# Strassen's seven products in a second group of tokens, weight sums taken from fp16, and two transposes copied out by ScalarE

## Chip, cores and metric

The kernel runs on one core of one Trainium2 chip. The metric is the time of one execution on the device, in microseconds (us). A core has TensorE (PE) for matmuls, VectorE (DVE), ScalarE (ACT) and GpSimd (POOL) for elementwise work, and SyncE (SP), which here only issues DMAs. Each engine works through its own queue in order.

## The reference

Two layers follow each other: a causal attention without softmax, with a decay per head, and a two-layer network with a gelu.

```python
# q, k, v: (4, 8, 768, 64); blocks of 64 positions, a state kv per head
intra = einsum('bhic,bhjc->bhij', qb, kb) * Dmask
out   = einsum('bhij,bhjd->bhid', intra, vb) + einsum('bhid,bhde->bhie', qb * lam_pow, kv_state)
kv_state = lam_block * kv_state + einsum('bhsd,bhse->bhde', kb_dec, vb)
# x: the attention's output as (3072, 512); w_in (512, 2048), w_out (2048, 512)
h = x @ w_in
g = gelu_tanh(h)
return g @ w_out            # (3072, 512), float32
```

## The kernel before, in words

**Attention in 24 steps.** A step is 256 positions of four heads of one batch. `prep(s)` scales q (DVE, L225), casts k (ACT, L230) and scales v (POOL, L215) into fp16. `stage_t(s)` transposes q and k on PE (L246) and copies the PSUM tile to SBUF: on ACT for steps 1, 5 and 6 (L253), half and half for 2 and 3, on DVE for 0, 4, 7 and 8 (L255). From step 9 on, a DMA transposes, and `stage_t` does nothing. `R(n, s)` computes the scores of step n (L275), then K-state and output products of n and s (L310, L324, L333), copies the output to `xT` on ACT (L352), masks the scores on DVE (`causal`, L284) and updates the state: `t` on DVE (L372 or L369), from which POOL makes `u` (L379). `U(n)` is the second update of a step.

**The network in 7 groups.** A superblock is two steps, 256 tokens. Groups are `[0,1], [2], [3], [4,5], [6,7], [8,9], [10,11]`: group 0 has 512 tokens, groups 1 and 2 have 256, the others 512. The first product (L407, in group 0 also L522) makes 128 columns of h at a time, and ACT writes their gelu to `gT` (L411). For the second product there are two forms. `mm2` (L422, groups 0 and 1) is the plain one: sixteen matmuls of 512 columns for each 128 tokens. `product` (L476, groups 2 to 6) is Strassen's scheme: tokens, the hidden dimension and the output columns are each halved, and seven products of sums take the place of eight, each of eight matmuls of 256 columns for each 128 tokens of a half. Its inputs are five sums of `gT` blocks (`sum_g`, DVE, L452), five sums of w_out blocks made once (`sum_wout`, DVE, L123), and plain blocks. Products come in the order 3, 4, 5, 2, 1, 7, 6; 3 and 4 need no sum of g. After product 2, ACT copies PSUM out (L483, L484) and DVE combines (L487, L488); after 1 and 6, DVE adds to it (L496, L508), and SP sends the rows out.

**The order is written out by hand.** `pin` keeps program order on every engine. `queue_group` (called in `R` when a group's last step is done) appends pieces of a group to the list `filler`: a piece is one `mm1` call, one `mm2` call or one `product`. `fill(n)` emits the next n pieces, so that attention steps and pieces alternate; the calls from L606 on set where. `behind(k, i0, i1)` hangs `sum_g` for rows i0 to i1 on piece k of a group, in program order just after it. Group 1's pieces (eight of `mm1`, eight of `mm2`) come out from the `fill(1)` behind `prep(8)` to the `fill(3)` of the loop's n = 9; group 2's follow.

**Weights.** w_out is loaded as fp32 into four staging tiles (tag `w32`, which the sums of g use later), cast to `w_out16` by POOL and ACT (`cast_wout`), and `sum_wout` reads the fp32 staging tiles: the half j = 0 before `fill(8)`, the half j = 1 in the loop at n = 8, 9 and 10.

Of the kernel before, what the change touches and what calls it, by code (L numbers as in the profile page):

```python
# [15 lines left out]
def kernel(  # L16
# [11 lines left out]
    pin = tc.keep_in_program_order  # L28
# [32 lines left out]
    def load_step(s):  # L61
# [3 lines left out]
        for nm, src in (("q", q), ("k", k), ("v", v)):  # L65
# [8 lines left out]
    w_out16 = w16p.tile([P, NF, DM], FP16)  # L74


    HF, HE = NF // 2, DM // 2
    w_sum16 = w16p.tile([P, 5, HF, HE], FP16)
    W_SUMS = {3: ((0, 1), ALU.subtract, (1, 1)), 4: ((1, 0), ALU.subtract, (0, 0)),
              1: ((0, 0), ALU.add, (1, 1)), 7: ((1, 0), ALU.add, (1, 1)),  # L80
              6: ((0, 0), ALU.add, (0, 1))}
    w_slot = {m: i for i, m in enumerate(W_SUMS)}
    wstage = {}
# [25 lines left out]
    def cast_wout(j, eng):  # L109
        t = wstage[("o", j)]  # L110
        for i in range(2):
            dst = w_out16[:, 4 * j + 2 * i : 4 * j + 2 * i + 2, :]
            src = t[:, 2 * i : 2 * i + 2, :]
            if eng[i] is nc.scalar:
                pin(nc.scalar.activation(out=dst, in_=src, func=AF.Copy))
            else:
                pin(nc.gpsimd.tensor_copy(out=dst, in_=src))

    def sum_wout(j, m, eng):

        (f0, e0), op, (f1, e1) = W_SUMS[m]
        a, b = wstage[("o", j + 2 * f0)], wstage[("o", j + 2 * f1)]
        pin(eng.tensor_tensor(w_sum16[:, w_slot[m], 4 * j : 4 * j + 4, :],  # L123
                              a[:, :, e0 * HE : e0 * HE + HE], b[:, :, e1 * HE : e1 * HE + HE], op))


    lam_in = const.tile([P, H], FP32)
# [74 lines left out]
    def prep(s):  # L202
        prep_qk(s)
        prep_v(s)
# [8 lines left out]
    def prep_v(s):  # L213
        tv = a16p.tile([P, 2, HH, D], FP16, tag="v16", name=f"v16_{s}")
        pin(nc.gpsimd.tensor_tensor(wide(tv[:]), ld32[s][2][:], decay(dv, s), ALU.mult))  # L215
        a16[s] = a16[s] + (tv,)
        if s >= 6:
            load_ahead(s + 3)

    def prep_qk(s):  # L220
        q32, k32, _ = ld32[s]
        tqk = a16p.tile([P, 2, 2, HH, D], FP16, tag="qk16", name=f"qk16_{s}")
        tq, tk = tqk[:, 0], tqk[:, 1]
        q_eng = nc.gpsimd if s == 3 else nc.vector
        pin(q_eng.tensor_tensor(wide(tq), q32[:], decay(dq, s), ALU.mult))  # L225
        if s == 0:
            inverse(halves[0])
            odd(halves[1])
            inverse(halves[1])
        pin(nc.scalar.activation(out=wide(tk), in_=k32[:], func=AF.Copy))  # L230
        a16[s] = (tq, tk)
        if s >= FIRST_DMA_T:
            o = qkp.tile([P, 2, 2, 2, P], FP16, tag="qkT", name=f"qkT_{s}")
            pin(nc.sync.dma_start_transpose(out=o[:].rearrange("p a j h t -> p (a j h) t"),
                                            in_=tqk[:].rearrange("p a j h d -> p (a j h d)")))
            qkT[s] = o

    def stage_t(s):
        if s >= FIRST_DMA_T:
            return  # L240
        tq, tk = a16[s][:2]
        Tps = ps_M.tile([P, 2, 2, 2, P], FP16, tag="M", name="Tps")
        for i, t in enumerate((tq, tk)):
            for hp in range(2):
                for j in range(2):
                    pin(nc.tensor.transpose(Tps[:, i, j, hp, :], t[:, j, 2 * hp : 2 * hp + 2, :],  # L246
                                            ident[:]))
        o = qkp.tile([P, 2, 2, 2, P], FP16, tag="qkT", name=f"qkT_{s}")
        if s in (2, 3):
            pin(nc.scalar.activation(out=o[:, 0], in_=Tps[:, 0], func=AF.Copy))  # L250
            pin(nc.vector.tensor_copy(out=o[:, 1], in_=Tps[:, 1]))
        elif s in (1, 5, 6):
            pin(nc.scalar.activation(out=o[:], in_=Tps[:], func=AF.Copy))  # L253
        else:
            pin(nc.vector.tensor_copy(out=o[:], in_=Tps[:]))  # L255
        qkT[s] = o
# [131 lines left out]
    filler = []  # L388

    def queue_group(g):  # L390
        N = len(groups[g]) * SB
        NTAU = N // P
# [10 lines left out]
        def mm1(fs):  # L403
            Hps = ps_M.tile([P, per, N], FP32, tag="M", name="Hps")
            for i, f in enumerate(fs):
                for c in range(NC):
                    pin(nc.tensor.matmul(by_block(Hps[:, i, :]), w_in16[:, c, f * P : (f + 1) * P],  # L407
                                         x(c), start=(c == 0), stop=(c == NC - 1)))
            f = fs[0]
            dst = gT[:, f, :, :] if per == 2 else gT[:, f % HF, f // HF : f // HF + 1, :]  # L410
            pin(nc.scalar.activation(out=dst, in_=Hps[:], func=AF.Gelu_apprx_tanh))  # L411
# [4 lines left out]
        def mm2(tau, part):  # L416

            if not O2.get(tau):
                O2[tau] = [ps_M.tile([P, DM], FP32, tag="M", name="O2ps"), 0]
            for f in range(4 * part, 4 * part + 4):  # L420
                n = O2[tau][1]
                pin(nc.tensor.matmul(O2[tau][0][:], gT[:, f % HF, f // HF, tau * P : (tau + 1) * P],  # L422
                                     w_out16[:, f, :], start=(n == 0), stop=(n == NF - 1)))
                O2[tau][1] += 1
            if O2[tau][1] < NF:
                return
            o32 = otp.tile([P, DM], FP32, tag="o32", name="o32")
            pin(nc.scalar.activation(out=o32[:], in_=O2.pop(tau)[0][:], func=AF.Copy))
            pin(nc.sync.dma_start(out=out[row0 + tau * P : row0 + tau * P + P, :], in_=o32[:]))
# [11 lines left out]
        def block(T, F, i):  # L441
            return gT[:, i, F, T * HN : (T + 1) * HN]

        def sum_g(i0, i1):
            for m, ((T0, F0), op, (T1, F1)) in G_SUMS.items():
                if m not in gsum:
                    k = len(gsum)
                    if k % 2 == 0:
                        pairs.append(wst.tile([P, 2, HF, HN], FP16, tag="w32", name=f"gs_{g}_{m}"))
                    gsum[m] = pairs[-1][:, k % 2]  # L450
                i = slice(i0, i1)
                pin(nc.vector.tensor_tensor(gsum[m][:, i, :], block(T0, F0, i), block(T1, F1, i), op))  # L452
# [92 lines left out]
        for i in range(HF):  # L545
            for fs in ([[i, i + HF]] if per == 2 else [[i], [i + HF]]):
                filler.append(lambda fs=fs: mm1(fs))
        if g == 1:
            for tau in range(NTAU):
                for part in (0, 2, 1, 3):  # L550
                    filler.append(lambda tau=tau, part=part: mm2(tau, part))
            return
        ms = ((3, 4, 5, 2), (1, 7, 6))
        order = [(m, p) for p in range(HN // P) for m in ms[0] + ms[1]]
        if g == len(groups) - 1:
# [1 line left out]
        for m, p in order:  # L557
            filler.append(lambda m=m, p=p: product(m, p))

        def behind(k, i0, i1):  # L560

            piece = filler[at + k]

            def both():
                piece()
                sum_g(i0, i1)

            filler[at + k] = both

        at = len(filler) - len(range(HN // P)) * 7 - HF * (2 // per)  # L570
        n1 = HF * (2 // per)
        if per == 2:
            behind(5, 0, 4)
            behind(n1, 4, 8)
        else:
            behind(9, 0, 4)
            behind(13, 4, 6)
            behind(n1, 6, 8)
# [7 lines left out]
    def fill(n):  # L586
        for _ in range(min(n, len(filler))):
            filler.pop(0)()

    def R(n, s):  # L590
        if n is not None:
            scores(n)
        products(n, s)
        if n is not None:
            causal(n)
        if s is not None and s % 2 == 1:
            g, i = group_of[s // 2]
            if i == len(groups[g]) - 1 and g > 0:
                queue_group(g)
        if n is not None:  # L600
            update(n, 0)

    def U(n):
        update(n, 1)
# [58 lines left out]
        cast_win(j)  # L663
    DVE, ACT, POOL = nc.vector, nc.scalar, nc.gpsimd
    cast_wout(0, (POOL, POOL))
    for m in W_SUMS:
        sum_wout(0, m, DVE)
    fill(8)
    cast_wout(2, (ACT, ACT))
    cast_wout(1, (POOL, ACT))  # L670
    cast_wout(3, (POOL, ACT))
    fill(9)
    prep(4)
    stage_t(4)
    prep(5)
    fill(2)
    R(4, None)
    stage_t(5)
# [4 lines left out]
    stage_t(6)  # L683
    U(5)
    prep(7)
    fill(2)
    R(6, 5)
    U(6)
# [1 line left out]
    prep(8)  # L690
    fill(1)
    stage_t(7)
    fill(2)
    R(7, 6)
    U(7)
# [3 lines left out]
    for n in range(8, NSTEP + 1):  # L699
        m = n if n < NSTEP else None  # L700
        if m is not None:
            stage_t(n)
        if n + 2 < NSTEP:
            prep(n + 2)
        fill(2 if n <= 12 else 4)
        R(m, n - 1)
        fill(1)
        if m is not None:
            U(m)
        for p in {8: (3, 4), 9: (1, 7), 10: (6,)}.get(n, ()):  # L710
            sum_wout(1, p, DVE)
        fill(2 if n == 11 or n > 12 and n % 2 else 3)
    fill(len(filler))

# [28 lines left out]
```

## Time and profile before

| what | value |
|---|---|
| median of 7 runs | 205.56 us (204.86 to 205.95) |
| profiled execution | 205.25 us, its span 203.5 us (1.75 us lie outside the span) |
| TensorE clock granted | 0.999 of full speed |
| busy: PE, DVE, ACT, POOL | 195.5, 145.7, 108.1, 70.0 us |
| gelu L411, mean of one | 596 ns |
| k cast L230, mean of one | 624 ns |
| ACT copy of a transposed step L253 | 1023 ns |
| DVE copy of a transposed step L255 | 691 ns |
| fp32 sum of weights L123, mean of one | 1362 ns (two tiles read), 1527 ns (one tile read) |

Durations in a row are those of whole instructions; the next instruction of the same queue can start a little before the end of the one ahead, so the timeline's starts are the better clock. "Idle before" is the time the engine stood still ahead of an instruction, with what ended it. The chain of work that ended last says which engine the end of the program hangs on at each moment.

### The profile page before, as it was taken

The page shows a single profiled execution, that of the slowest core. Times are in us where ns is not written, and L with a number is a line of the kernel's source. Part 1 is how long each engine was busy: PE and PEld are TensorE (multiplying, and loading weights), DVE is VectorE, ACT ScalarE, POOL GpSimd, SP SyncE. Part 2 cuts the span into 40 slices and gives each one's busy share as a digit, 9 for nine tenths or more (in the row PEclk, how much of TensorE's full clock was granted, in tenths as well). Part 3 has the DMA queues.
Part 4 walks back from the last instruction along what each step waited for, and adds up shares of the span by engine and source line. Part 5 has one row for each costly group of instructions (what it writes and reads, how often), then busy time and mean ns, then how long its engine had stood idle before and what let it go on. Part 6 is the DMA issues. An engine that isn't in the chain of part 4 may idle for free.

```text
span 203.5 us, 5595 instructions
## 1 busy us (share of the span) xinstructions
PE 195.5 (96%) x2325; PEld 127.5 (63%) x2325; DVE 145.7 (72%) x275; ACT 108.1 (53%) x204; POOL 70.0 (34%) x80
## 2 busy tenths in 40 slices
PE   7689999999999999999999999999999999999993
PEld 2356544556875798644688654788554788544882
DVE  4998727877699998929997828996739773226652
ACT  3265678475873573477722387641576431666210
POOL 5496123646586851336134404315412101000000
PEclk9999999999999999999999999999999999999999
DMA  5999999999999999896669993648340003300014
GB/s 158 297 314 388 388 387 377 288 286 319 341 265 230 291 247 150 208 292 170 48 172 229 236 253 105 153 108 134 87 97 0 0 3 103 108 0 0 3 47 160
DMA packets 63937, 37.85 MB, mean 186 GB/s; under 512 B 17576, under 2 KB 59048, under 8 KB 63912
## 3 DMA queue, kind: packets, MB, share of 16 engines
q1 hardware_dynamic: 63616, 37.23, 71.0%
q8 instruction: 18, 0.29, 0.6%
q10 hardware_dynamic: 296, 0.26, 0.4%
q14 instruction: 7, 0.06, 0.1%
HBM read 27.26 MB, written 6.29 MB: 165 GB/s over the span
## 4 chain that ended last, share of the span: by engine, by line
PE 89%; DMA 3%; SPq 3%; DVE 2%; ACT 1%; issue 1%
PE Hps L407 37%; PE O2ps L422 10%; PE MB L476 8%; PE MA L476 7%; PE MD L476 7%; PE MC L476 4%; PE Hps L522 3%; PE Sps L275 3%; PE OK L333 3%; PE OK L324 3%; DMA k<-in_k_dram 3%; SPq L68 3%; PE Tps L246 1%; PE OK L310 1%; DVE t L372 1%
## 5 line engine op out<-in xcount | busy, mean ns | idle before, releaser
L407 PE MATMUL Hps<-xT,w_in 128*128 128x512 f16 (+1 forms) x416 | 79.1, 346 | 0.0
L411 ACT ACTIVATE gT<-Hps 128x512 f16<-128x512 f32 x88 | 52.4, 596 | 22.9 <-PE Hps L407 22.1
L407 PEld LDWEIGHTS <-w_in 128*128 128x128 f16 x416 | 40.2, 98 | 33.5
L379 POOL TENSOR_TENSOR u<-t,lumask 128x256 f16<-128x256 f32 x40 | 31.3, 789 | 79.7 <-DVE t L372 53.1
L452 DVE TENSOR_TENSOR gs<-gT 128x512 f16<-128x512 f16 (+1 forms) x70 | 36.6, 586 | 10.8 <-ACT gT L411 10.6
L284 DVE TENSOR_TENSOR PT<-Sps,mask 128x1024 f16<-128x1024 f32 x24 | 29.2, 1216 | 16.9 <-PE Sps L275 16.8
L476 PEld LDWEIGHTS <-gs 128*128 128x128 f16 x360 | 34.9, 98 | 4.0
L215 POOL TENSOR_TENSOR v<-v,dv 128x512 f16<-128x512 f32 x24 | 29.2, 1218 | 4.9 <-DMA v<-in_v_dram 3.3
L352 ACT ACTIVATE xT<-OK 128x256 f16<-128x256 f32 x47 | 18.1, 453 | 19.6 <-PE OK L333 16.0
L422 PE MATMUL O2ps<-w_out,gT 128*128 128x512 f16 x96 | 21.9, 379 | 0.0
L230 ACT ACTIVATE qk<-k 128x512 f16<-128x512 f32 x24 | 15.0, 624 | 8.6 <-DMA k<-in_k_dram 8.6
L225 DVE TENSOR_TENSOR qk<-q,dq 128x512 f16<-128x512 f32 x23 | 19.2, 834 | 0.0
L483 ACT ACTIVATE m<-MB 128x512 f32<-128x512 f32 x9 | 5.4, 597 | 25.4 <-PE MB L476 25.4
L476 PE MATMUL MA<-w_sum,gT 128*128 128x256 f16 x144 | 17.5, 273 | 0.1
L476 PE MATMUL MD<-w_sum,gs 128*128 128x256 f16 x136 | 17.5, 273 | 0.0
L476 PE MATMUL MB<-w_out,gs 128*128 128x256 f16 x144 | 17.2, 273 | 0.0
L476 PEld LDWEIGHTS <-gT 128*128 128x128 f16 x144 | 14.0, 98 | 2.8 <-ACT gT L411 0.3
L422 PEld LDWEIGHTS <-gT 128*128 128x128 f16 x96 | 9.2, 98 | 9.9
L487 DVE TENSOR_TENSOR o<-MA,m 128x512 f32<-128x512 f32 x9 | 6.2, 689 | 12.7 <-ACT m L483 12.7
L372 DVE SCALAR_TENSOR_TENSOR t<-t,lamu,OK 128x64 f32<-128x64 f32 x64 | 14.6, 272 | 0.7
L275 PEld LDWEIGHTS <-qkT 64*64 64x64 f16 x384 | 6.1, 106 | 8.5 <-issue 4.4
L123 DVE TENSOR_TENSOR w_sum<-wo,wo 128x1024 f16<-128x1024 f32 x6 | 7.9, 1362 | 4.2 <-DMA wo<-in_moe_w_out_dram 4.2
(59 smaller groups left out, 168.2 us busy)
## 6 DMA issues: line engine op xcount, KB each, us to landing
q<-in_q_dram SPq DMA_DIRECT2D x24, 256.0 KB, 4.9
k<-in_k_dram SPq DMA_DIRECT2D x24, 256.0 KB, 5.0
v<-in_v_dram SPq DMA_DIRECT2D x24, 256.0 KB, 5.1
out_dram<-o SPq DMA_DIRECT2D x22, 256.0 KB, 4.3
wo<-in_moe_w_out_dram SPq DMA_DIRECT2D x4, 1024.0 KB, 9.5
wi<-in_moe_w_in_dram SPq DMA_DIRECT2D x4, 512.0 KB, 7.0
wi<-in_moe_w_in_dram SPq DMA_DIRECT2D x2, 1024.0 KB, 11.6
out_dram<-o SPq DMA_DIRECT2D x2, 128.0 KB, 1.9
```

Of the source, the lines that this page charges most:

```text
L215: pin(nc.gpsimd.tensor_tensor(wide(tv[:]), ld32[s][2][:], decay(dv, s), ALU.mult))
L225: pin(q_eng.tensor_tensor(wide(tq), q32[:], decay(dq, s), ALU.mult))
L230: pin(nc.scalar.activation(out=wide(tk), in_=k32[:], func=AF.Copy))
L284: pin(nc.vector.tensor_tensor(t[:].rearrange("p a b c d -> p (a b) (c d)"), Ss.pop(n)[:].rearrange("p a b c d -> p (a b) (c d)"), mask[:]. ...
L352: pin(nc.scalar.activation(out=d, in_=o, func=AF.Copy))
L372: pin(nc.vector.scalar_tensor_tensor(t[:, hp, :], state[half][:, hp, :], lamu[:, 2 * half + hp : 2 * half + hp + 1], K[:, hp, :], ALU.mult ...
L379: pin(nc.gpsimd.tensor_tensor(u[:], state[half][:].unsqueeze(2).to_broadcast([P, 2, 2, D]), lumask[:, 2 * half : 2 * half + 2, :].unsqueez ...
L407: pin(nc.tensor.matmul(by_block(Hps[:, i, :]), w_in16[:, c, f * P : (f + 1) * P], x(c), start=(c == 0), stop=(c == NC - 1)))
L411: pin(nc.scalar.activation(out=dst, in_=Hps[:], func=AF.Gelu_apprx_tanh))
L422: pin(nc.tensor.matmul(O2[tau][0][:], gT[:, f % HF, f // HF, tau * P : (tau + 1) * P], w_out16[:, f, :], start=(n == 0), stop=(n == NF - 1)))
L452: pin(nc.vector.tensor_tensor(gsum[m][:, i, :], block(T0, F0, i), block(T1, F1, i), op))
L476: pin(nc.tensor.matmul(dst, lhsT, rhs, start=(i == 0), stop=(i == HF - 1), skip_group_check=True))
```

## The change

Four things are done together.

1. Group 1 takes `product` instead of `mm2`: 7 pieces instead of 8. Its gelu output gets five sums of its own.
2. In groups 1 and 2 the sums of g come one product at a time: 5 and 2 for the first half of the rows behind the sixth `mm1` piece, the second half of 5 behind the last `mm1`, of 2 behind product 3, all of 1, 7 and 6 behind products 4, 5 and 2. That makes seven instructions (four of 512 elements, three of 1024) where group 2 had ten of 512.
3. `sum_wout` reads `w_out16` (fp16) instead of the staging tiles. So it comes after the casts: five of half 0 and one of half 1 behind them, the other four behind `prep(5)`, `prep(7)` and `stage_t(7)`.
4. The transposes of steps 7 and 8 are copied out by ACT. At n = 8 the last `fill` takes two pieces instead of three.

```diff
     def sum_wout(j, m, eng):
 
         (f0, e0), op, (f1, e1) = W_SUMS[m]
-        a, b = wstage[("o", j + 2 * f0)], wstage[("o", j + 2 * f1)]
-        pin(eng.tensor_tensor(w_sum16[:, w_slot[m], 4 * j : 4 * j + 4, :],
-                              a[:, :, e0 * HE : e0 * HE + HE], b[:, :, e1 * HE : e1 * HE + HE], op))
+
+        def rows(f, e):
+            f = f * HF + 4 * j
+            return w_out16[:, f : f + 4, e * HE : e * HE + HE]
+
+        pin(eng.tensor_tensor(w_sum16[:, w_slot[m], 4 * j : 4 * j + 4, :], rows(f0, e0), rows(f1, e1), op))
...
-        elif s in (1, 5, 6):
+        elif s in (1, 5, 6, 7, 8):
             pin(nc.scalar.activation(out=o[:], in_=Tps[:], func=AF.Copy))
...
-        def sum_g(i0, i1):
+        def sum_g(i0, i1, ms=None):
             for m, ((T0, F0), op, (T1, F1)) in G_SUMS.items():
+                if ms and m not in ms:
+                    continue
...
-        if g == 1:
-            for tau in range(NTAU):
-                for part in (0, 2, 1, 3):
-                    filler.append(lambda tau=tau, part=part: mm2(tau, part))
-            return
...
         if per == 2:
-            behind(5, 0, 4)
-            behind(n1, 4, 8)
+            behind(5, 0, 4, (5, 2))
+            behind(7, 4, 8, (5,))
+            behind(8, 4, 8, (2,))
+            behind(9, 0, 8, (1,))
+            behind(10, 0, 8, (7,))
+            behind(11, 0, 8, (6,))
...
     cast_wout(0, (POOL, POOL))
-    for m in W_SUMS:
-        sum_wout(0, m, DVE)
     fill(8)
     cast_wout(2, (ACT, ACT))
     cast_wout(1, (POOL, ACT))
     cast_wout(3, (POOL, ACT))
+    for m in (6, 3, 4, 1, 7):
+        sum_wout(0, m, DVE)
+    sum_wout(1, 6, DVE)
     fill(9)
     prep(4)
     stage_t(4)
     prep(5)
+    sum_wout(1, 3, DVE)
     fill(2)
...
     prep(7)
+    sum_wout(1, 4, DVE)
     fill(2)
...
     stage_t(7)
+    sum_wout(1, 1, DVE)
+    sum_wout(1, 7, DVE)
     fill(2)
...
-        for p in {8: (3, 4), 9: (1, 7), 10: (6,)}.get(n, ()):
-            sum_wout(1, p, DVE)
-        fill(2 if n == 11 or n > 12 and n % 2 else 3)
+        fill(2 if n in (8, 11) or n > 12 and n % 2 else 3)
```

More of the change, by code (lines that the diff above doesn't have):

```diff
@@ L558, in queue_group, with behind @@
             filler.append(lambda m=m, p=p: product(m, p))
-        def behind(k, i0, i1):
+        def behind(k, i0, i1, ms=None):
             piece = filler[at + k]
@@ L565, in both @@
                 piece()
-                sum_g(i0, i1)
+                sum_g(i0, i1, ms)
             filler[at + k] = both
```

## The prediction

> **What bounds the kernel now.** I read the page first (busy shares, chain of work that ended last), then the chain in order of time around group 1, then the timelines of DVE, POOL and ACT there.
>
> ```profile
> PE 195.5 (96%) x2325; PEld 127.5 (63%) x2325; DVE 145.7 (72%) x275; ACT 108.1 (53%) x204; POOL 70.0 (34%) x80
> ...
> PE 89%; DMA 3%; SPq 3%; DVE 2%; ACT 1%; issue 1%
> ```
>
> PE is the bound: 89% of the chain is PE, and what isn't lies almost wholly in the first 16 us and the last 3. The chain in order of time (start, length, what):
>
> ```profile
> 53.41 0.35 PE Sps L275 x16
> ...
> 59.18 0.87 PE Hps L407 x8
> 60.05 4.32 PE O2ps L422 x20
> ...
> 65.39 2.59 PE O2ps L422 x12
> 67.98 2.62 PE Hps L407 x24
> ```
>
> The reader is to see that one PE piece follows another without a gap, and that group 1's second product (the O2ps lines, 32 matmuls) takes 4.32 + 2.59 = 6.91 us, with step 9's attention (1.03 us) between. So PE work taken out is worth its full length, and any new wait of PE costs its full length. DVE over the same stretch:
>
> ```profile
> 55.75 0.78 DVE L225 TENSOR_TENSOR qk<-q,dq 128x512 f16<-128x512 f32 x1
> ...
> 57.16 1.39 DVE L225 TENSOR_TENSOR qk<-q,dq 128x512 f16<-128x512 f32 x1
> ...
> 60.60 2.99 DVE L123 TENSOR_TENSOR w_sum<-wo,wo 128x1024 f16<-128x1024 f32 x2
> 63.51 1.52 DVE L225 TENSOR_TENSOR qk<-q,dq 128x512 f16<-128x512 f32 x1
> ```
>
> and POOL:
>
> ```profile
> 55.37 1.63 POOL L379 TENSOR_TENSOR u<-t,lumask 128x256 f16<-128x256 f32 x2 [2.39 <-DVE t L369]
> 56.97 2.49 POOL L215 TENSOR_TENSOR v<-v,dv 128x512 f16<-128x512 f32 x2
> 60.34 2.17 POOL L379 TENSOR_TENSOR u<-t,lumask 128x256 f16<-128x256 f32 x2 [0.89 <-DVE t L372]
> 62.47 2.02 POOL L215 TENSOR_TENSOR v<-v,dv 128x512 f16<-128x512 f32 x1
> ```
>
> DVE is busy without a break from 56.5 us on, and its q scaling takes 1.39 and 1.52 us where it takes 0.68 with POOL idle. Today nobody waits for that: the masks and sums made here are due much later.
>
> **What the Trainium skill says.** (1) "SBUF — State Buffer", section "Who interferes with whom": a DVE instruction with two SBUF inputs and a GpSimd one that reads SBUF exclude each other for the whole instruction; the second blocks. The trace agrees: the q scaling at 63.51 ends at 65.03, 0.54 us after POOL's v (62.47 + 2.02 = 64.49). (2) "VectorE: DVE Perf Modes", section "The perf-mode tier table": an addition of two 16-bit SBUF tensors runs at twice the fp32 rate. Trace: five fp16 sums of 1024 elements below take 3.10 us, 0.605 each; the fp32 one at 72.76 took 1.21 us. (3) "TensorE: Matmul & The Clock Gate", section "Back-to-back issue gap": 262 cycles for 256 columns, 518 for 512, so 109 against 216 ns. Trace: 0.87 us for 8 of 256 (109 ns), 6.91 for 32 of 512 (216 ns).
>
> The timeline of the sums of g, free (181 us) and beside POOL (73.9 us, where POOL runs one u and one v):
>
> ```profile
> 73.90 3.02 DVE L452 TENSOR_TENSOR gs<-gT 128x512 f16<-128x512 f16 x5
> ...
> 181.60 3.10 DVE L452 TENSOR_TENSOR gs<-gT 128x1024 f16<-128x1024 f16 x5 [6.84 <-ACT gT L411]
> 185.05 1.76 DVE L452 TENSOR_TENSOR gs<-gT 128x512 f16<-128x512 f16 x5 [0.36 <-ACT gT L411]
> ```
>
> A sum of 512 costs 0.335 us (five in 1.76, 0.08 of it the last one's tail), of 1024 0.605. One v of POOL costs the DVE instruction behind it 1.52 - 0.68 = 0.85 us, one u the rest of 3.02 - 1.76 = 1.26, 0.42. DVE and POOL take turns: each DVE sum lets one POOL instruction in.
>
> **The change part by part.**
>
> *PE.* 32 matmuls of 512 columns (6.91 us) go, 7 x 8 of 256 come (7 x 0.874 = 6.12). **Saved: 0.79 us**, all on the path. Nothing else on PE changes.
>
> *Weight sums.* Ten fp32 sums (6 x 1.36 + 4 x 1.53 = 14.3 us of DVE) become ten of 0.605 (6 us). Of the first six, five wait for ACT's cast of w_out rows 8 to 11 (done 35.05). From there: these five and q of step 4 (5 x 0.605 + 0.60 = 3.6) plus one blocked by the POOL cast that runs from 37.3 (0.85) and 0.45 for the one from 34.5: 35.1 + 4.9 = 40.0, where q is ready at 39.88 today and PE takes it at 39.95. I put that at nothing; bounds 0 and +0.15, no gain since PE doesn't wait there now. The last four lie in gaps of DVE (0.5 to 1.4 us idle before each mask) and cost nothing before 54 us. The DVE time won lies at 60 to 73 us.
>
> *Transpose 7 on ACT.* The ACT timeline today:
>
> ```profile
> 51.50 0.62 ACT L230 ACTIVATE qk<-k 128x512 f16<-128x512 f32 x1
> 52.02 1.15 ACT L411 ACTIVATE gT<-Hps 128x512 f16<-128x512 f32 x2
> ```
>
> The copy comes between the two gelus: it starts at 52.52 and lasts 1.02 (L253), ends 53.54, seen by PE at 53.60. PE's scores of step 7 are due at 53.41 (chain). **Cost: 0.20 us** of PE; bounds 0 (if ACT's k cast comes half a us earlier) and 0.3. Copy 8 starts at 57.0 and ends 58.0, scores 8 are due 58.46: free. The gelu of the last `mm1` comes at 60.29 + 0.60, so product 3's last matmul waits about **0.10 us**.
>
> *DVE from 55.95 us on (55.75 today + 0.20).* PE now needs sums of g at once. In program order, with POOL's turns (u of step 7, v of 9 and 10, u of 8 twice, v of 11):
>
> | DVE work | own | POOL's turn | done |
> |---|---|---|---|
> | q 9, q 10 | 0.70, 0.60 | 0.35 | 57.60 |
> | sums 5, 2, first halves | 2 x 0.335 | 2 x 0.85 | 59.97 |
> | mask 8, t | 1.14, 0.39 | | 61.50 |
> | sum 5 second half | 0.335 | | 61.84 |
> | t, sum 2 second half | 0.39, 0.335 | 0.20 | 62.76 |
> | sum 1 | 0.605 | 0.42 | 63.79 |
> | q 11 | 0.60 | 0.85 | 65.24 |
> | sum 7 | 0.605 | | 65.84 |
> | combine L487, L488 | 2 x 0.60 | | 67.04 |
> | sum 6 | 0.605 | | 67.65 |
>
> PE, with product 3 starting at 59.89 + 0.20 (59.89 is the first O2ps matmul today): product 4 at 61.07, 5 at 61.94, 2 at 62.82, attention 63.69, 1 at 64.72, 7 at 65.60, 6 at 66.47. Sums 5, 2 and 1 are in time by 0.1 to 1 us. Sum 7 is 0.3 late, and **sum 6, at 67.65 + 0.08 tail + 0.06 to be seen = 67.79, is 1.32 us late** (sum 7's wait is inside this). Product 6 ends at 68.66, and group 2's first matmul starts there; today at 67.82. Net: **+0.84 us** = -0.79 + 0.20 + 0.10 + 1.32, to rounding. Bounds of the sum-6 wait: 0 if no POOL turn falls in the row, 1.7 if u of step 8 blocks a full turn more.
>
> *What queues behind.* Mask 9 and the updates come after sum 6 (mask done 68.8, needed at 70.6; PSUM slots of step 9 free by 70.3, reused at 71.5): in time. SP's two output DMAs now wait for L508 (about 70.8) ahead of step 12's transposing DMA, which waits for q 12 there anyway; it is needed at 82. PSUM: the two banks of group 1 return with L488. Group 2's sums: seven instead of ten; its product 6 has step 12's attention before it and finds sum 6 ready by 0.1 to 0.3 us: nothing, bounds 0 and +0.3. Evacuation: two ACT copies (0.60 + 0.38) for two of 0.59, hidden.
>
> **Sum.** The profiled execution is 205.25 us (span 203.5 + 1.75 outside it): 206.09. It lies 0.31 below the median of the runs, so on the median's scale 205.56 + 0.84 = **206.4**.
>
> **Rivals.** *A, the forecast*: DVE and POOL take strict turns, product 6 waits 1.3 us: 206.4, own range 205.9 to 206.8. For it: every blocked row fits the 0.85 and 0.42. Against it: it needs both v turns between 57.4 and 60 us to fall between sums. *B, half of it*: POOL's v of 9 and 10 come earlier or behind the first sums, so that sum 5's second half starts with the gelu at 60.95; only u and v 11 (1.47 us) delay the row, product 6 waits 0.77: -0.79 + 0.30 + 0.77 = +0.3: 205.85. *C, the other side*: POOL's instructions miss the row altogether; then sum 6 is bound by ACT's copy behind product 2 (64.56 + 1.20 + 0.69 = 66.45) and comes just in time. The gain is 0.79 - 0.30 = 0.5 (205.1), or 0.79 if copy 7 isn't late either (204.8). It decides from POOL turns in the row of under 0.7 us in all. *That the change doesn't do what it says* (PE columns not removed) is excluded by the counts.
>
> **Numbers.** Chances: A 0.50, B 0.26, C 0.24. I take 0.3% (0.6 us) as what a measurement can tell from no change. Slower by more: 0.42 of A, 0.04 of B: 0.46. Faster by more: only C without the late copy, 0.16. Within: 0.38. The range 204.95 to 206.85 leaves out half of C (0.12) and the end of A (0.07).
>
> **What would show it.** Chain of waits: PE products of group 1 in 6.1 us of matmul time plus a wait for DVE gs ahead of the last one (1.3 us in A, 0.8 in B, none in C). PE wait for ACT qkT at 53.4 of 0.2. DVE's sums of group 1 with single instructions of about 1.2 to 1.5 us where POOL runs. I am wrong if these are all 0.4 and 0.7 us long, or if PE waits in group 2 or at step 4.

## The result, and the profile after

The changed kernel takes 206.6 us (median of 13 runs, 205.98 to 207.36) against 205.26 for the kernel before beside it (34 runs): ratio 1.0062, 95% interval 1.0047 to 1.0078, which is 1.0 to 1.6 us more. A second comparison in another session gave 206.44 against 205.45, ratio 1.0054 (95% interval 1.0034 to 1.0074). It is **slower**, as forecast. That the forecast time, 206.4, is so close is in part luck: it was the kernel before at 205.56 and 0.84 more, but beside the changed kernel the kernel before took 205.26. The forecast difference, 0.84, lies under the interval of the first comparison and inside that of the second. Its profiled execution took 206.33 us (span 204.5), that of the kernel before 205.25 (203.5).

The page of the changed kernel (busy time and share by engine; then the chain of work that ended last):

```profile
PE 195.6 (96%) x2349; PEld 129.5 (63%) x2349; DVE 145.7 (71%) x281; ACT 109.1 (53%) x206; POOL 67.1 (33%) x80
...
PE 80%; DMA 5%; SPq 4%; DVE 4%; ACT 3%; issue 2%; ACTq 0%
```

The busy totals hardly move; what moves is the chain, which now leaves PE for DVE, ACT and a DMA. Which PE instructions wait, after 17 us (total, times, longest):

```profile
PE MD L481 <- DVE gs L457: 0.8, 1, 0.8
PE Sps L278 <- ACT qkT L256: 0.2, 1, 0.2
```

The PE timeline (start, length; MA holds products 4 and 3, MD products 7 and 6):

```profile
53.74 0.42 PE L278 MATMUL Sps<-qkT 64*64 64x128 f16 x16 [0.20 <-ACT qkT L256]
...
60.29 2.01 PE L481 MATMUL MA<-w_sum,gT 128*128 128x256 f16 x16
...
64.91 1.04 PE L481 MATMUL MC<-w_sum,gs 128*128 128x256 f16 x8
66.05 1.05 PE L481 MATMUL MD<-w_sum,gs 128*128 128x256 f16 x8
67.84 1.05 PE L481 MATMUL MD<-w_sum,gs 128*128 128x256 f16 x8 [0.75 <-DVE gs L457]
68.72 2.78 PE L410 MATMUL Hps<-xT,w_in 128*128 128x256 f16 x24
```

Eight matmuls of a product take 0.875 us to the next start. Product 7 starts at 66.05 where 64.91 + 0.875 = 65.78 was due: 0.27 late. Product 6 starts at 67.84 where 66.92 was due: 0.92 late. (The printed idle of 0.75 is less, since the end of the matmul ahead is counted with its 0.17 us of tail.) DVE and POOL at the same time:

```profile
57.87 2.44 DVE L457 TENSOR_TENSOR gs<-gT 128x512 f16<-128x512 f16 x2
60.24 1.21 DVE L287 TENSOR_TENSOR PT<-Sps,mask 128x1024 f16<-128x1024 f32 x1
...
63.86 1.53 DVE L228 TENSOR_TENSOR qk<-q,dq 128x512 f16<-128x512 f32 x1
65.31 0.68 DVE L457 TENSOR_TENSOR gs<-gT 128x1024 f16<-128x1024 f16 x1
...
67.11 0.67 DVE L457 TENSOR_TENSOR gs<-gT 128x1024 f16<-128x1024 f16 x1
```

```profile
57.37 2.67 POOL L218 TENSOR_TENSOR v<-v,dv 128x512 f16<-128x512 f32 x2
...
63.35 1.49 POOL L218 TENSOR_TENSOR v<-v,dv 128x512 f16<-128x512 f32 x1
```

Two sums of 512 elements, 0.75 us by themselves, take 2.44 beside two v; sum 6 ends at 67.78 and PE sees it at 67.84.

**Counting without the start.** Until 25 us all the kernels here have the same code, and yet the first 512-column matmul of line 407 (410 in the changed kernel) starts anywhere from 25.07 to 26.43 us in their profiled executions. From group 3's first matmul to the last instruction of the chain it is 115.87 us before and after. So the traces are compared over the stretch between these two points: 84.23 - 25.49 = 58.74 us before, 85.14 - 25.44 = 59.70 after, **+0.96**. It splits: 0.18 at the transposes of step 4 (from the first O2ps matmul to group 1's first matmul 17.96 us instead of 17.78), 0.27 at the scores of step 7 (3.43 instead of 3.16 from there), 0.50 from the first matmul of group 1's second product to group 2's first (8.43 instead of 7.93). The last is -0.79 of work, +0.09 at product 3, +0.27 and +0.92 at products 7 and 6.

The first wait ends when q of step 4 does, on DVE; PE's transposes follow:

```profile
35.07 4.56 DVE L127 TENSOR_TENSOR w_sum<-w_out 128x1024 f16<-128x1024 f16 x5 [2.94 <-ACT w_out L115]
39.55 0.68 DVE L228 TENSOR_TENSOR qk<-q,dq 128x512 f16<-128x512 f32 x1
```

```profile
40.29 0.62 PE L249 MATMUL Tps<-ident,qk 128*128 128x128 f16 x8
```

The second ends with ScalarE's copy of step 7's transposes ("copy 7"). Ahead of it in ScalarE's queue stands the copy of an output, which waits for a DMA:

```profile
51.17 0.60 ACT L431 ACTIVATE o<-O2ps 128x512 f32<-128x512 f32 x1 [0.87 <-DMA out_dram<-o]
...
52.66 1.03 ACT L256 ACTIVATE qkT<-Tps 128x1024 f16<-128x1024 f16 x1
```

### The profile page after: what moved, and what is told of

Its sections match the earlier page's. It is cut to its first block, busy times and chain, and to the rows that moved or that the text cites. A ratio compares the mean times of both kernels' runs of the same rounds, so it can differ in the third digit from the quotient of the medians.

```text
span 204.5 us, 5655 instructions
## 1 busy us (share of the span) xinstructions
PE 195.6 (96%) x2349; PEld 129.5 (63%) x2349; DVE 145.7 (71%) x281; ACT 109.1 (53%) x206; POOL 67.1 (33%) x80
## 4 chain that ended last, share of the span: by engine, by line
PE 80%; DMA 5%; SPq 4%; DVE 4%; ACT 3%; issue 2%; ACTq 0%
PE Hps L410 34%; PE MD L481 8%; PE MB L481 8%; PE MA L481 7%; PE O2ps L425 5%; SPq L68 4%; PE MC L481 4%; PE Hps L527 3%; DMA wi<-in_moe_w_in_dram 3%; PE Sps L278 3%; PE OK L336 3%; DMA out_dram<-o 2%; PE OK L327 2%; DVE gs L457 1%; ACT gT L414 1%
## 5 line engine op out<-in xcount | busy, mean ns | idle before, releaser
L382 POOL TENSOR_TENSOR u<-t,lumask 128x256 f16<-128x256 f32 x40 | 29.1, 733 | 82.0 <-DVE t L375 60.4
L457 DVE TENSOR_TENSOR gs<-gT 128x512 f16<-128x512 f16 (+1 forms) x74 | 42.3, 628 | 12.7 <-ACT gT L414 12.6
L481 PEld LDWEIGHTS <-gs 128*128 128x128 f16 x400 | 38.5, 98 | 5.8 <-DVE gs L457 1.4
L481 PE MATMUL MD<-w_sum,gs 128*128 128x256 f16 x152 | 19.6, 273 | 0.9 <-DVE gs L457 0.8
L481 PE MATMUL MA<-w_sum,gT 128*128 128x256 f16 x160 | 19.5, 273 | 0.1
L481 PE MATMUL MB<-w_out,gs 128*128 128x256 f16 x160 | 19.1, 273 | 0.0
L481 PEld LDWEIGHTS <-gT 128*128 128x128 f16 x160 | 15.5, 98 | 3.1 <-ACT gT L414 0.5
L425 PE MATMUL O2ps<-w_out,gT 128*128 128x512 f16 x64 | 14.6, 379 | 0.0
L127 DVE TENSOR_TENSOR w_sum<-w_out 128x1024 f16<-128x1024 f16 x10 | 9.6, 997 | 6.4 <-POOL w_out L117 3.5
L278 PE MATMUL Sps<-qkT 64*64 64x128 f16 x384 | 10.0, 222 | 0.9 <-DVE qkT L254 0.5
```

Of the source, the lines that this page charges most:

```text
L278: pin(nc.tensor.matmul(Sps[half64(c), hl, hp, jk, :], o[half64(hl), 1, jk, hp, half64(c)], o[half64(hl), 0, :, hp, half64(c)], start=True, ...
L382: pin(nc.gpsimd.tensor_tensor(u[:], state[half][:].unsqueeze(2).to_broadcast([P, 2, 2, D]), lumask[:, 2 * half : 2 * half + 2, :].unsqueez ...
L481: pin(nc.tensor.matmul(dst, lhsT, rhs, start=(i == 0), stop=(i == HF - 1), skip_group_check=True))
```

## Experiments

The first two rows are the changed kernel itself, the others edits of it. Ratios are to the kernel before, measured beside each. "DVE's row" is DVE's work for group 1 in the order of its queue, from the q scaling of step 9 to sum 6.

| kernel | stretch, us (before: 58.74) | wait at step 4 | at scores 7 | at products 4 to 6 in all | ratio, 95% |
|---|---|---|---|---|---|
| changed | 59.70 | 0.18 | 0.27 | 1.18 | 1.0062, 1.0047 to 1.0078 |
| changed, again | 59.34 | 0 | 0 | 1.28 | 1.0054, 1.0034 to 1.0074 |
| plain group 1 | 58.96 | 0.21 | 0 | | 1.0029, 1.0011 to 1.0048 |
| v without reads | 58.41 | 0 | 0.35 | 0 | 0.9996, 0.9979 to 1.0014 |
| v 11 twice | 62.23 | 0.36 | 1.77 | 2.03 | 1.0126, 1.0099 to 1.0152 |
| sum 6 ahead | 58.86 | 0.18 | 0.36 | 0.27 | 1.0012, 0.9997 to 1.0026 |
| two early waits | 59.67 | 0 | 0 | 1.60 | 1.0038, 1.0017 to 1.0058 |
| sums 1 and 7 earlier | 59.58 | 0 | 0.33 | 1.19 | 1.0045, 1.0026 to 1.0065 |
| row only | 59.24 | 0.19 | 1.01 | 0 | 1.0007, 0.9991 to 1.0024 |
| own output tile | 58.43 | 0.39 | 0 | 0 | 0.9982, 0.9961 to 1.0003 |
| all waits out | 58.12 and 58.11 | 0 | 0 | 0.06 | 0.9987, 0.9967 to 1.0006; 0.9983, 0.9960 to 1.0007 |
| DVE copies 7, 8 | 58.52 | 0 | 0 | 0.46 | 1.0006, 0.9979 to 1.0033 |

A wait is what a section of PE's timeline takes over its length before (the first two columns), or over the 7.25 us that group 1's products and step 9's attention take with only the 0.09 at product 3. The section "at step 4" goes from the first O2ps matmul to group 1's first, "at scores 7" from there to the scores of step 7; where step 7's transposes were moved from the second to the first, the two are taken together.

The two early waits go with the start. Seven profiles have copy 7 and the sixth weight sum where the changed kernel has them, and the shared output tile. In the four whose first 512-column matmul starts at 25.07 to 25.50 us, the two waits come to 0.45 to 2.13 us; in the three that start at 26.17 to 26.43, to 0 to 0.35. With both moved out, starts of 25.13 and 26.18 us give the same stretch to 0.01 us. So the stretch of a kernel with early waits also depends on how early its execution started, and the column of the products is the one to compare.

**The changed kernel again.**

> The changed kernel as it is, beside the next three on one chip, so that their differences are taken within one session. Both theories: 0.9 to 1.3 us over the kernel before, about 206.3; product 6 of group 1 waits 0.9 us.

1.1 us over the kernel before by the ratio. In its profile neither early wait is there and the stretch is 0.60 longer: the early waits differ from execution to execution, those of the products hardly do (1.18 and 1.28).

**Plain group 1.** The products in group 1 alone undone:

```diff
+        if g == 1:
+            for tau in range(NTAU):
+                for part in (0, 2, 1, 3):
+                    filler.append(lambda tau=tau, part=part: mm2(tau, part))
+            return
...
-        fill(2 if n in (8, 11) or n > 12 and n % 2 else 3)
+        fill(2 if n == 11 or n > 12 and n % 2 else 3)
```

> Group 1 takes its plain second product again (32 matmuls of 512 columns); the fp16 weight sums, the sums of g one product at a time in group 2 and the copies of transposes 7 and 8 on ScalarE stay. Theory (four waits of PE: 0.13 us at the transposes of step 4, 0.27 at the scores of step 7, 0.1 at product 3 and 1.2 at products 7 and 6 of group 1, against 0.79 us of PE work saved): only the first two waits are left and the saving is gone too, so 0.4 us over the kernel before, about 205.65. Rival (the moved weight sums and copies cost the time, not the Strassen products): as slow as the changed kernel, 206.3 or more.

Ratio 1.0029, 0.6 us over the kernel before (0.2 to 1.0); the theory had 0.4, the rival the 1.1 to 1.3 of the changed kernel. So about half of the loss by the clock does not need the Strassen products at all; what is left in this kernel are the moved sums and copies and the new order of sums in group 2, whose section takes 16.42 us for 16.41. In the profile only 0.21 of it is seen, and not at the transposes of step 4, which are in time: it is at the products with step 4's u.

```profile
46.82 0.60 PE L336 MATMUL OK<-qkT,u 128*128 128x128 f16 x4
```

Before, these took 0.40. Mask 4 starts on DVE at 44.42 us, 0.6 after its scores are done, since a moved weight sum stands ahead of it and takes 1.53 us beside POOL's v of step 5; the updates and u follow that mask. The prediction had put these sums into gaps of DVE at no cost.

**v without reads.** POOL fills three v instead of computing them:

```diff
-        pin(nc.gpsimd.tensor_tensor(wide(tv[:]), ld32[s][2][:], decay(dv, s), ALU.mult))
+        if s in (9, 10, 11):
+            pin(nc.gpsimd.memset(tv[:], 0.0))
+        else:
+            pin(nc.gpsimd.tensor_tensor(wide(tv[:]), ld32[s][2][:], decay(dv, s), ALU.mult))
```

> The changed kernel, but POOL fills the scaled v of steps 9, 10 and 11 with a constant instead of computing it from v (these values are left out), so that three POOL instructions near group 1's sums no longer read SBUF. DVE's own work is the same. Theory (DVE's row of sums is late because three v and some u of POOL take turns with it, 0.85 us for each v): the row is 2.5 us shorter, sum 6 then ends at about 66.6 behind ScalarE's copy, product 6 doesn't wait, product 7 neither: 1.2 us less than the changed kernel, about 205.1, 0.1 to 0.2 below the kernel before. Rival (DVE's own work alone makes the row late): no change, product 6 still waits 0.9 us.

Its timelines of DVE and POOL, and the products on PE:

```profile
58.51 0.75 DVE L460 TENSOR_TENSOR gs<-gT 128x512 f16<-128x512 f16 x2
```

```profile
57.98 0.98 POOL L219 MEMSET v<- 128x512 f16 x2
```

```profile
66.41 1.92 PE L484 MATMUL MD<-w_sum,gs 128*128 128x256 f16 x16
```

The same two sums of g take 0.75 us although POOL is busy beside them for 0.45 us: here it only writes. Products 7 and 6 run in one go. The rival (DVE's own work) falls: that work is unchanged, and the wait of 1.18 is gone.

**v 11 twice.** The opposite, one turn more:

```diff
+        if s == 11:
+            pin(nc.gpsimd.tensor_tensor(wide(tv[:]), ld32[s][2][:], decay(dv, s), ALU.mult))
         a16[s] = a16[s] + (tv,)
```

> The changed kernel in which POOL scales v of step 11 twice (the second pass writes the same values again). Theory of the turns: one more POOL instruction that reads SBUF falls between q 11 and sum 7, so sums 7 and 6 end 0.85 us later, product 7 waits 1.1 and product 6 still 0.9: 0.85 over the changed kernel. Rival (DVE's own work makes the row late): no change to the changed kernel.

```profile
67.05 1.52 DVE L459 TENSOR_TENSOR gs<-gT 128x1024 f16<-128x1024 f16 x1
```

Sum 7 takes 1.52 us instead of 0.68, product 7 waits 1.12 instead of 0.27 (its PE timeline: 66.64 + 0.875 = 67.51 due, 68.63 taken), product 6 still 0.92: 2.03 for 1.18, the 0.85 expected. The time rose by more (207.92 against 206.44), since this profile shows another wait that I had not put down to this edit:

```profile
55.48 0.42 PE L280 MATMUL Sps<-qkT 64*64 64x128 f16 x16 [1.69 <-ACT qkT L258]
```

It lies ahead of anything that the edit touches in the queues, and is taken up below with the output tile. How much of the clock's excess is due to it no run shows.

**Sum 6 ahead of the combination.**

```diff
-            behind(10, 0, 8, (7,))
-            behind(11, 0, 8, (6,))
+            behind(10, 0, 8, (7, 6))
```

> The changed kernel with sum 6 of groups 1 and 2 behind product 5, together with sum 7, and so ahead of the two combining DVE instructions. Theory: sum 6 of group 1 ends 1.2 us earlier, at 66.6, product 6 is due at 66.9: its wait of 0.9 us goes, that of product 7 (0.27) stays. The bank that group 2's first matmul takes comes back 0.6 us later, at 67.8, just when it is due: 0 to 0.2 us. Sum: 0.7 to 0.9 below the changed kernel, about 205.5. Rival (DVE simply has too much work up to 69 us, whatever its order): the wait only moves to group 2's first matmuls, and the time stays within 0.2 us.

```profile
65.42 1.28 DVE L457 TENSOR_TENSOR gs<-gT 128x1024 f16<-128x1024 f16 x2
```

```profile
66.16 1.92 PE L481 MATMUL MD<-w_sum,gs 128*128 128x256 f16 x16
67.92 2.78 PE L410 MATMUL Hps<-xT,w_in 128*128 128x256 f16 x24
```

Products 7 and 6 are one stretch from 66.16, group 2's first matmul comes at 67.92 without a wait (66.16 + 2 x 0.875 = 67.91), and only product 7's 0.27 is left. Ratio 1.0012, against 1.0062 and 1.0054 of the changed kernel in other sessions. The place of sum 6 ahead of the two combining instructions was worth the 0.92.

**The two early waits moved out.**

```diff
-    sum_wout(1, 6, DVE)
     fill(9)
...
     prep(6)
+    sum_wout(1, 6, DVE)
     fill(2)
...
+    stage_t(7)
     fill(1)
     prep(8)
     fill(1)
-    stage_t(7)
```

> The changed kernel with the transposes of step 7 (and ScalarE's copy of them) one piece and one prep earlier, ahead of the last piece of group 0, and the sixth weight sum (half 1 of sum 6) behind the prep of step 6 instead of ahead of that of step 4. Theory: the PE waits of 0.13 us at the transposes of step 4 and of 0.27 at the scores of step 7 go, and DVE's row for group 1 starts 0.4 earlier with them: 0.4 us below the changed kernel, about 205.9; product 6 still waits 0.9. Rival (the row of DVE is bound by something that doesn't move, such as loads): the two waits go but product 6 waits 1.3, and the time is that of the changed kernel.

The waits went, as the theory said, but DVE's row did not start earlier: the waits of the products rose to 1.60, and nothing was won. My expectation failed here. Its DVE timeline shows why:

```profile
52.43 2.55 DVE L127 TENSOR_TENSOR w_sum<-w_out 128x1024 f16<-128x1024 f16 x2
54.90 1.21 DVE L287 TENSOR_TENSOR PT<-Sps,mask 128x1024 f16<-128x1024 f32 x1
```

Scores 7 are done at 54.43 (54.01 + 0.42), but mask 7 starts at 54.90, right behind two weight sums that take 2.55 us for 1.3 beside one u of POOL and its v of step 8. I had said that these lie in gaps. They do only while the scores are late.

**Weight sums 1 and 7 earlier.** That cause was tried, on top of the last kernel:

```diff
     sum_wout(1, 4, DVE)
+    sum_wout(1, 1, DVE)
+    sum_wout(1, 7, DVE)
...
-    sum_wout(1, 1, DVE)
-    sum_wout(1, 7, DVE)
```

> The kernel with the two early waits moved out, and besides with the second halves of weight sums 1 and 7 behind the prep of step 7, so that they no longer stand ahead of mask 7 on DVE. The theory formed after that kernel's run (its DVE row did not start earlier because these two sums, one of them behind the turn of v 8, held mask 7 back by 0.45 us): mask 7 now starts with its scores, sums 7 and 6 come 0.4 to 0.5 us earlier, products 7 and 6 wait 1.1 instead of 1.5 us together, and the stretch from the first 512-column matmul of the plain part of group 0 to group 3 is 0.4 to 0.5 us shorter than there: 59.2 us instead of 59.67. Rival (the row is held by something else, the loads or v 9 and 10): mask 7 starts with its scores but sums 7 and 6 end where they did, 59.6 or more.

Mask 7 starts with its scores and the products wait 1.19 instead of 1.60, the 0.41 expected. But the stretch shrinks by 0.09 only: the rest is given back on PE ahead of it, where the third matmul piece of group 1 now waits for a PSUM bank that step 6's update holds, since mask 6 stands behind the moved sums:

```profile
52.65 1.03 PE L410 MATMUL Hps<-xT,w_in 128*128 128x256 f16 x8 [0.17 <-DVE t L372]
```

From group 0's last piece to scores 7 it takes 0.3 us more than in the kernel it is made from.

**The row alone, and with a tile for the last output.** Both take sum 6 ahead and move the prep of step 11 behind group 1's products:

```diff
-        if n + 2 < NSTEP:
+        if n + 2 < NSTEP and n != 9:
             prep(n + 2)
...
+        if n == 9:
+            prep(11)
```

The second gives the last output of group 0 a tile that nothing else uses yet:

```diff
-            o32 = otp.tile([P, DM], FP32, tag="o32", name="o32")
+            if g == 0 and tau == 3:
+                o32 = mtp.tile([P, 3 * HE], FP32, tag="m525", name="m525")[:, 0:DM]
+            else:
+                o32 = otp.tile([P, DM], FP32, tag="o32", name="o32")
```

> The changed kernel with sum 6 behind product 5 and the prep of step 11 behind group 1's products; the two early waits (transposes of step 4, scores of step 7) stay. Theory: the waits of products 7 and 6 go, 0.4 to 0.5 us of early waits and 0.1 at product 3 stay against 0.79 saved: 0.2 to 0.3 under the kernel before, about 205.2, and 0.4 over the kernel with all waits out. Rival (the early waits cost nothing by themselves, since another queue is as late): as fast as the one with all waits out.

> The changed kernel with sum 6 behind product 5 and the prep of step 11 behind group 1's products, and with a tile of its own for the last output of group 0, so that ScalarE's copy of it doesn't wait until an earlier output DMA has landed. Theory (copy 7 is late because it stands behind that wait in ScalarE's queue, and the wait changes from run to run with the DMAs): the scores of step 7 wait 0 to 0.05 us, and the time is 0.4 us or more under the same kernel without the tile, near the one with all waits out, about 205.0 to 205.2. Rival (copy 7 is late because ScalarE's own work ahead of it is too long): the scores wait 0.3 to 0.9 as there.

In both the products wait for nothing, so the row theory holds. The scores of step 7 wait 1.01 in the first, more than the early waits of 0.4 to 0.5 expected for it, and not at all in the second. ScalarE's timeline, in the first kernel:

```profile
51.55 0.60 ACT L431 ACTIVATE o<-O2ps 128x512 f32<-128x512 f32 x1 [1.61 <-DMA out_dram<-o]
52.04 0.62 ACT L233 ACTIVATE qk<-k 128x512 f16<-128x512 f32 x1
52.56 0.59 ACT L414 ACTIVATE gT<-Hps 128x512 f16<-128x512 f32 x1
53.04 1.03 ACT L256 ACTIVATE qkT<-Tps 128x1024 f16<-128x1024 f16 x1
```

and in the second:

```profile
50.36 0.60 ACT L434 ACTIVATE m<-O2ps 128x512 f32<-128x512 f32 x1 [0.21 <-PE O2ps L425]
```

The copy of group 0's last output stands ahead of copy 7 in ScalarE's queue, and it waits until the first output DMA has landed and given its tile back. Where the profiles show it waiting for that, it started between 51.01 and 51.83 us; in the kernel with v 11 twice it started at 52.91, 2.37 us idle, which the profile puts down to a PE instruction done long before. With a tile of its own it starts at 50.36 and copy 7 is in time. The ratios of the two (0.9982 against 1.0007) were taken in different sessions and their intervals overlap, so what the tile is worth is read from one profile of each, not from the clock. Each can be set beside the kernel with all waits out (below) in its own session: 1.0007 beside 0.9987 without the tile, 0.9982 beside 0.9983 with it, as expected, but within the intervals.

**All waits out.** Sum 6 ahead, step 11's prep later, and the two early moves together.

> The changed kernel with sum 6 behind product 5, the whole prep of step 11 (q, k, v and their DMAs) behind group 1's products, the transposes of step 7 ahead of the last piece of group 0, and the sixth weight sum behind the prep of step 6. Theory (each wait belongs to its own cause, and DVE's row is the one that is late): q 11 and the turn of v 11 leave the row (1.45 us), sums 7 and 6 end 0.4 and 1 us before they are due, the two early waits are gone; what stays is 0.1 at product 3, so the saving of 0.79 us comes through: 0.6 to 0.7 under the kernel before, about 204.9, and 1.6 under the changed kernel. Rival (DVE's work only moves on: mask 9, the combination and q 11 make later products or step 11 wait): as slow as the kernel before, 205.5, with waits of PE between 68 and 80 us.

> The kernel with all waits out once more, with more rounds, since its first comparison with the kernel before could not tell a gain from none. Theory: the 0.6 us by which its trace is shorter from the first 512-column matmul on: 0.3% under the kernel before, about 204.9. Rival (the shorter stretch is given back before or after it): 205.5.

Both profiles have a stretch 0.62 and 0.63 us shorter than before; of the saving of 0.79 only 0.09 at product 3 and 0.06 at product 5 or 2 are missing. The ratios are 0.9987 and 0.9983, 0.3 us less, but both intervals reach past 1: that this version beats the kernel before is what the traces say and what the clock could not settle.

**Copies 7 and 8 by DVE.** The last kernel with the branch for ScalarE as it was, `elif s in (1, 5, 6)`.

> The kernel with all waits out, but transposes 7 and 8 are copied out by VectorE as in the kernel before. Theory: copy 7 now lies where VectorE is idle, copy 8 makes its row 0.6 us longer, and sums 7 and 6 were ready 1.0 and 1.2 us ahead of their products: no wait comes back and the time is that of the kernel with all waits out within 0.2 us. Rival (the row has no room for it): products 7 or 6 wait again, 0.3 us or more.

```profile
62.55 1.49 PE L481 MATMUL MB<-w_out,gs 128*128 128x256 f16 x12 [0.30 <-DVE gs L457]
```

Wrong by a little: the products wait 0.46 in all. I had looked at the room ahead of sums 7 and 6; the tight one is the second half of sum 5. In the kernel with all waits out it has no room at all:

```profile
61.41 0.41 DVE L457 TENSOR_TENSOR gs<-gT 128x512 f16<-128x512 f16 x1
```

```profile
61.37 1.99 PE L481 MATMUL MB<-w_out,gs 128*128 128x256 f16 x16
```

It ends at 61.82, and product 5's fifth matmul is due at 61.37 + 0.44 = 61.81. Counted from the scores of step 7, the copies make it 0.39 us later. Copy 7 is not free: mask 7 starts 1.14 us after these scores do, for 0.89, so 0.25 of the 0.39 is there before copy 8. The two copies were moved together, and no run shows what either costs alone.

## Why the prediction was right

By its own terms (predicted, then measured in the changed kernel's trace):

- *PE work*: -0.79. Without the waits of products 4 to 6, group 1's products and the attention between take 7.25 us for 7.93: 0.68, and 0.09 of product 3's wait: 0.77. Right.
- *Step 4's transposes*: put at nothing with 0.15 as the upper end. It was 0.18 in this profile, so the prediction's own sign of being wrong, a wait of PE at step 4, did show. **Mis-sized**: q of step 4 ends at 40.23, where the sum of rows said 40.0. Of the eight profiles that keep the sixth weight sum there, four have this wait, of 0.18 to 0.39; in *v 11 twice* q and k themselves came late from their DMAs, in *plain group 1* the loss is at a later place, and two have none. With that sum moved away none of five has it, three of these with an early start.
- *Copy 7*: 0.20 forecast, 0.27 measured. The mechanism (queued on ScalarE behind a gelu) was right and its upper end, 0.3, wrong: the output copy ahead waits for a DMA, and executions show 0 to 1.77 us of wait. The list of waits of the kernel before has it, 0.8 us of ScalarE's copy L428 for a DMA of `out`; it cost nothing then, as nothing that PE was about to need stood behind it.
- *Product 3*: 0.10 forecast, 0.09 measured.
- *The last four weight sums*: put into gaps at nothing. That held in the changed kernel's profile, by a little (mask 7 starts 0.05 us after its scores are done), and did not in *plain group 1* and *the two early waits moved out*, where such a sum held a mask up by 0.5 to 0.6.
- *DVE's row*: the forecast has mask 8 at 59.97, sum 7 done at 65.84, sum 6 seen at 67.79; measured 60.24, 65.91, 67.84. Products 7 and 6 wait 1.19 for 1.32 forecast. That the row is late through POOL's turns is shown from both sides: without v's reads no wait, with one v more 0.85 more.
- *Group 2*: forecast to wait for nothing new; from its first matmul to group 3's it takes 16.42 us against 16.41.

The sum: 0.84 forecast, 0.96 in the trace, 0.60 in its second profile. The clock says 1.3 (1.0 to 1.6) and 1.1 (0.7 to 1.5). That the rest comes from executions that start early and lose their lead again in the early waits, which the kernel before does not have, fits the spread of those waits over the profiles; but no run shows it for the timed executions themselves, and the kernel before has one profile only. The early waits were the part of the forecast that was too small: 0.20 in the prediction, 0.45 in this trace (0 in the second profile).

Of the rivals, B (half the turns) is out: both v turns of steps 9 and 10 fell on the first two sums, as the 2.44 us show. C's condition, POOL's instructions missing the row, is nearly what *v without reads* makes (only the turns of u are left), and there the products wait for nothing. C's outcome, the saving coming through, is what the kernel with all waits out shows in its trace, with two of the v turns still in the row.

## What to carry to other kernels

When an engine that was off the path becomes the supplier of the bound, write its queue down instruction by instruction, with the turns it must give to the engine that shares its reads, and compare each end with the moment it is due: the total of its busy time (145.7 us before and after) says nothing. And before something the bound needs is queued on an engine, look at what stands ahead of it there for a wait on a DMA: here that wait was free until then. A saving of 0.4% needs all of this to be in order at once; here the place of one sum among its neighbours cost 0.92 us, more than all of it.

## What the runs showed of the hardware

- DVE instructions with two SBUF inputs and POOL instructions that read SBUF took strict turns: each v of POOL (1.04 us alone) held one DVE sum up by 0.85 us, each u (0.61 alone) by 0.42, whatever the DVE instruction's own length (a sum of 1024 elements took 1.52 instead of 0.68). The page "SBUF — State Buffer" of the Trainium skill, section "Who interferes with whom", says that a GpSimd instruction that only writes does not collide; two memsets (0.98 us together) and two sums (0.75) that overlapped for 0.45 us agree, as the sums took no longer than alone.
- The start is less steady than the rest: with the same code, the first 512-column matmul of the plain part began between 25.07 and 26.43 us in fourteen profiled executions, while the last 115.87 us were the same to the hundredth in the kernel before and the changed one.
